# Four interleaved attention layers: VectorE's unspent allowance carried over, gates computed later, and some GpSimd copies moved to VectorE

## The chip, the cores and the metric

The kernel runs on one core of a Trainium2 chip. The metric is the device time of one execution in microseconds (us), lower is better. A core has five engines, each with its own queue, worked off in order: TensorE (PE, matmuls; its weight loads are listed as PEld), VectorE (DVE), ScalarE (ACT), GpSimd (POOL) and SyncE (SP, which here only issues DMA transfers). An instruction that needs another engine's result waits on a semaphore, and all that stands behind it in its queue waits too. TensorE writes to PSUM, eight banks of 128 x 512 fp32.

## What is computed

There are 2048 tokens of width 512, 32 heads of 16, and four residual layers in the order A, B, A, B, each on a layer norm of x.

```
B: q,k,v = x @ wqkv;  o = softmax(q k^T / 4) v over all 2048 keys;  o @ wo
A: four segments of 512 tokens, in each, per head:
     a_dot = softmax(q k^T / 4 + causal mask) v        (within the segment)
     a_mem = phi(q) M / (phi(q) z + 1e-6)              (memory of earlier segments)
     o = g * a_mem + (1 - g) * a_dot,   g = sigmoid(beta)
     M += phi(k)^T v ;  z += sum phi(k)
   o @ wo
phi(t) = t + 1 if t > 0 else exp(t)
```

In A the mask lets a query see only keys at or before its own position.

## The kernel before: how the work is laid out

All data stay on chip after the first loads. A planner in Python (class `Builder`) writes out the order of every engine's instructions before anything runs; a scheduler (`Sched`) adds the semaphore waits that the reads and writes need. Nothing is decided on the chip, so a change in the planner's rules moves instructions on all engines.

**A step.** The main loop (`attention`, L1189 on) advances in steps. A step takes up to three score tiles ("banks") of 128 keys x 512 queries, each of one head, from the groups that are selected. `unit` (L986) issues TensorE's score matmuls into PSUM banks 0 to 2 or 3 to 5, in turn, and one exponential on ScalarE for all three (L1039, PSUM to the SBUF tile pT). For A, GpSimd then zeroes what the causal mask forbids (L1054). Two steps later (three for A) TensorE multiplies pT with the values (`pv`, L1060) and adds into PSUM bank 6, the only accumulator. A group is the four heads of one residue and one 512-token query segment: 64 banks for B (fewer for partial key sets), 12 for A.

**The end of a group.** `finish` (L1081) has VectorE transpose the accumulator into the tile tT (L1099) or, for partial sums, copy or add it (L1090, L1092); only then may TensorE write bank 6 for the next group. VectorE takes reciprocals (L1103), in A it multiplies by the gate `omgT` (L1106), GpSimd scales the result into `ob` (L1112) and VectorE transposes that into `oT` (L1127).

**Masked queries.** A group's scores use a copy of the queries with the other heads' rows set to zero, the tile qm (L957). It is made when the group is selected, by VectorE for A groups and for groups that are needed at once, else by GpSimd.

**Exponentials on VectorE.** In addition to the three banks a step can take a fourth one for VectorE (`dx_pick`, L711): scores go to PSUM bank 7, VectorE converts them into fixed point (`dxt`, L748) and runs a chain of six instructions for one or two banks (`dx_chain`, L772 to L782) that gives the exponential's bits. At most total/6 banks of a group go this way (10 of 64), not in every step, and not while the planner's VectorE balance `cr_dve` is under -300.

**Background tasks and the balance.** Layer norm, projections, memory updates and output projections of other layers and segments run as generators between the steps (`background`). Each part names its cost, so many TensorE units and so many ns of VectorE. `credit` (L858) adds to the balances at each step: 1420 ns of VectorE for a step of B, 1300 for A, 2600 when work runs short. The balance is cut off at one step's amount, so what a step did not use is dropped.

**Memory and gates.** `task_mem` (L588) adds phi(k)^T v into M (L637, L639) and makes two copies masked per head, Mn and Mz (L643, L645, on GpSimd, 24 of each), which later matmuls read. `gates` (L421) computes the sigmoids gtok and omgT from beta: for each an exponential on ScalarE (L427) and two instructions on VectorE (L429, L430). It is called in the first segment's task (L553), behind the first layer norm and ahead of the first projections. The two small copies of beta are DMA transfers that SyncE issues behind the first weights (L381, L385).

TensorE's spare time is filled: `keep_busy` (L326) issues matmuls with a zero weight into bank 6, up to 1024 columns a step.

Of the kernel before, what the change touches and what calls it, by code (L numbers as in the profile page):

```python
# [5 lines left out]
ALU = mybir.AluOpType  # L6
# [168 lines left out]
def bcast(ap, dims):  # L175
    return bass.AP(tensor=ap.tensor, offset=ap.offset, ap=[list(ap.ap[0])] + [list(d) for d in dims])
# [36 lines left out]
class Builder:  # L213
# [326 lines left out]
    def task_A(self, L, s):  # L540
        sl = s % 2
        need = [("x", L, s)]
        if s >= 2:
            need += [("attn", L, s - 2), ("mem", L, s - 2)]
        if s == 0 and L > 0:
            need += [("attn", L - 2, 2), ("attn", L - 2, 3), ("mem", L - 2, 2), ("mem", L - 2, 3)]
        yield need, 0, 0
        k = yield from self.ln_part(L, s)
        yield ["xT"], 0, 0
        slot = self.take_xT()  # L550
        if L == 0 and s == 0:
            yield from self.ln_first(k, slot)
            self.gates()  # L553
        else:
            yield from self.ln_tiles(L, s, k, slot)
            yield [("dma", ("xT", L, s))], 0, 0
        for c in range(NCH):
            yield from self.proj_fm(self.wA, self.b_wA[1], 512, slot, c, self.KA[:, sl, c, :], self.b_KA[sl][c])
            self.flags.add(("K", L, s, c))
            yield from self.proj_fm(self.wA, self.b_wA[0], 0, slot, c, self.QA[:, sl, c, :], self.b_QA[sl][c])  # L560
            self.flags.add(("Q", L, s, c))
            if c == 0:
                for ti in range(4):
                    yield from self.proj_tm(self.wA, self.b_wA[2], 1024, slot, ti,
                                            self.v_evac(self.VA[:, sl, ti, :], self.b_VA[sl][ti]))
                self.flags.add(("V", L, s))
        if s < 3:
            prev = (L, s - 1) if s else (L - 2, 3)
            read = [("dma", ("amemT",) + prev + (3,))] if prev[0] >= 0 and prev[1] else []
            yield ([("mem",) + prev] if prev[0] >= 0 else []), 0, 0  # L570
            old = [o for b in self.b_phk for o in b.reads.values()]
            for c in range(NCH):
                self.dma_tr(self.phk[:, :, c * 128:(c + 1) * 128], self.KA[:, sl, c, :], [self.b_KA[sl][c]], [self.b_phkc[c]],
                            ("phk", L, s), old)
            for j in range(2):
                yield [("dma", ("phk", L, s))] + read, 0, 0
                a, ba = self.phk[:, 2 * j:2 * j + 2, :], self.b_phk[2 * j:2 * j + 2]
                yield from self.phi(a, self.b_phkc + ba, a, ba)
            self.flags.add(("phk", L, s))
        self.give_xT(slot)  # L580
        if s > 0:
            for c in (0, 2):
                yield [("op", L, s - 1), ("mem", L, s - 1)] + ([("dma", ("amemT", L, s - 1, 3))] if s > 1 else []), 0, 0
                yield from self.phi(self.QA[:, sl, c:c + 2, :], self.b_QA[sl][c:c + 2], self.phq[:, c:c + 2, :], self.b_phq[c:c + 2])
            self.flags.add(("phq", L, s))
        self.flags.add(("proj", L, s))

    def task_mem(self, L, s):  # L588
# [33 lines left out]
        if s < 3:  # L622
            for j in range(2):
                yield [("phk", L, s), ("V", L, s)], 2, 450
                bank, al = self.misc(), self.new_alloc()
                for cc in range(2):
                    c = 2 * j + cc
                    o = bank.col0 + cc * 136
                    for ti in range(4):
                        self.mm(self.ps[:, o:o + 136], self.phk[:, ti, c * 128:(c + 1) * 128],  # L630
                                self.VA[:, sl, ti, c * 136:(c + 1) * 136], ti == 0, ti == 3,
                                [self.b_phk[ti], self.b_VA[sl][ti]], bank, al)
                src = self.ps[:, bank.col0:bank.col0 + 272].rearrange("p (c h f) -> p c h f", c=2, f=17)
                M = self.M[:, 2 * j:2 * j + 2, :, :]
                bM = [self.b_M[j]]
                if s == 0:
                    self.op("dve", (lambda M, src: lambda e: e.tensor_copy(M, src))(M, src), writes=bM, bank=bank, alloc=al)  # L637
                else:
                    self.op("dve", (lambda M, src: lambda e: e.tensor_tensor(M, M, src, ALU.add))(M, src), reads=bM, writes=bM,  # L639
                            bank=bank, alloc=al)  # L640
            for c in range(NCH):
                hn = bcast(self.hmask[:, 0:1], [[1, 8], [0, 16]])
                self.op("pool", (lambda c, hn: lambda e: e.tensor_tensor(self.Mn[:, c, :, :], self.M[:, c, :, 0:16], hn, ALU.mult))(c, hn),  # L643
                        reads=[self.b_M[c // 2], self.b_hm], writes=[self.b_Mn])
                self.op("pool", (lambda c: lambda e: e.tensor_tensor(self.Mz[:, c, :], self.M[:, c, :, 16], self.hmask[:, :], ALU.mult))(c),  # L645
                        reads=[self.b_M[c // 2], self.b_hm], writes=[self.b_Mz])
        self.flags.add(("mem", L, s))

# [209 lines left out]
    def credit(self, pe, dve):  # L858

        self.cr_pe = min(self.cr_pe + pe, pe)  # L860
        self.cr_dve = min(self.cr_dve + dve, dve)

    def background(self, bank=None):
        while self.cr_dve > 0 and self.cr_pe > 0:
# [66 lines left out]
    def select(self, late):  # L931
        tail = self.sel[-2:]
        if len(self.sel) > 2 and self.seqA and self.seqA[0][0].L and all(g.kind == "B" and not g.pos for g in tail) and self.met(self.group_needs(self.seqA[0][0])):

            for g in tail:
                self.sel.remove(g)
                self.qm_free.insert(0, g.qm)
            self.seqB.insert(0, tail)
        while len(self.qm_free) > 1 and (len(self.sel) <= 1 or len(self.sel) == 2 and all(g.kind == "B" and g.total < 64 for g in self.sel)):
            pair = None  # L940
            for seq in (self.seqA, self.seqB):
                if seq and self.met(self.group_needs(seq[0][0])):
                    pair = seq.pop(0)
                    break
            if pair is None and self.seqB and sum(len(g.banks) - g.pos for g in self.sel) <= 6 and self.split():
                pair = self.seqB.pop(0)
            if pair is None:
                return
            for g in pair:
                g.qm = self.qm_free.pop(0)  # L950
                isA = g.kind == "A"
                q = (self.QA[:, g.qseg % 2, g.c, :] if isA else self.QB[:, g.qseg, g.c, :])
                bq = (self.b_QA[g.qseg % 2][g.c] if isA else self.b_QB[g.qseg][g.c])
                m = self.qm[:, g.qm, :]
                col = self.par[:, g.e:g.e + 1]
                eng = "dve" if late or isA else "pool"
                self.op(eng, (lambda m, q, col: lambda e: e.tensor_scalar(m, q, col, 0.0, op0=ALU.mult, op1=ALU.add))(m, q, col),  # L957
                        reads=[bq, self.b_par], writes=[self.b_qm[g.qm]])
                self.sel.append(g)
# [121 lines left out]
    def finish(self, g):  # L1081
# [20 lines left out]
        br = self.b_rd[m]  # L1102
        self.op("dve", lambda e: e.reciprocal(rd, tT[:, :, 16]), reads=[bt], writes=[br])  # L1103
        if g.kind == "A":
            om = self.omgT[:, g.c, g.e:g.e + 1]
            self.op("dve", lambda e: e.tensor_scalar(rd, rd, om, None, op0=ALU.mult), reads=[br, self.b_omgT], writes=[br])  # L1106
        if g.e == 0:
# [62 lines left out]
    def attention(self):  # L1170
# [18 lines left out]
        while True:  # L1189
# [23 lines left out]
            isA = items[0][0].kind == "A"  # L1213
# [5 lines left out]
            self.cr_dve -= self.pv_step(n)  # L1219
            self.run_deferred(False)  # L1220
            self.background(False if split else None)
            if self.step > 10:
                self.keep_busy()
            self.bg_cols = 0
# [49 lines left out]
```

## Time and profile before

| | us |
|---|---|
| three timed runs, median (lowest, highest) | 2142.66 (2138.74, 2143.29) |
| profiled execution, its own time | 2140.73 |
| its span, first to last instruction | 2138.6 |
| ScalarE busy | 2007.1 |
| TensorE matmuls busy | 1797.9 |
| VectorE busy | 1591.0 |
| GpSimd busy | 404.8 |
| ScalarE waited for TensorE before exponentials (L1039) | 88.3 |
| VectorE waited for TensorE before dxt (L748) | 88.1 |
| TensorE matmuls waited for tT (L1099), 51 times | 29.8 |
| TensorE matmuls waited for qm on GpSimd, 3 times | 8.3 |
| mean granted TensorE clock | 0.966 |

How to read it: in a group's line stand line of code, engine, operation, output<-input with shapes, count, then busy us and mean ns of one, then the engine's idle time ahead of these and whom it waited for. In a timeline the columns are start in us, duration, engine, line, operation, and in square brackets the idle time before it with its releaser; "x5" means that several instructions are drawn together, and the duration is then the stretch that they cover. In a table of windows each row is a stretch (start:end, length), then busy us and number of instructions of PE, PEld, DVE, ACT and POOL, then the granted TensorE clock as a share of full speed, the DMA engines' busy share and GB/s. Records of successive instructions of an engine can overlap, so the sum of the durations can exceed the busy time.

### The profile page before, as it was taken

The numbers are of one execution on the slowest core, as the hardware profiler recorded it, in microseconds if no ns is written. First come the engines' busy times: TensorE is split into PE (matmuls) and PEld (weight loads), VectorE is DVE, ScalarE is ACT, GpSimd is POOL, SyncE is SP. The second block draws the span as 40 slices with busy tenths as digits, with TensorE's granted clock in tenths as the row PEclk, the third lists the DMA queues.
The fourth block names the chain that finished last, engine by engine and source line by source line (L and its number), as shares of the span: only waits on it lengthen the run. The fifth ranks groups of instructions, "written<-read, shape, count | busy, mean of one in ns | idle before, by whom it ended". The sixth has DMA issues, their size and how long they took to land.

```text
span 2138.6 us, 34960 instructions
## 1 busy us (share of the span) xinstructions
PE 1797.9 (84%) x13626; PEld 497.4 (23%) x13726; DVE 1591.0 (74%) x2806; ACT 2007.1 (94%) x1618; POOL 404.8 (19%) x833
## 2 busy tenths in 40 slices
PE   7788888878888988889888888888888888888887
PEld 3222222222222222222222222222222222222222
DVE  6665665487658885688857975548899999989996
ACT  5689998999989999899998999999999999999997
POOL 3532533020150002400033102401100000000000
PEclk9899999999999999899988999999999999999999
DMA  4011100000000000000000001000000000000000
GB/s 138 11 30 21 21 11 11 11 1 13 9 1 11 1 13 9 11 11 1 16 11 6 1 1 21 11 11 1 11 1 1 1 11 1 1 1 11 1 1 11
DMA packets 67142, 24.81 MB, mean 12 GB/s; under 512 B 59808, under 2 KB 66464, under 8 KB 66976
## 3 DMA queue, kind: packets, MB, share of 16 engines
q1 hardware_dynamic: 66976, 22.57, 4.7%
q8 instruction: 108, 1.77, 0.3%
q14 instruction: 58, 0.48, 0.1%
HBM read 6.30 MB, written 2.10 MB: 4 GB/s over the span
## 4 chain that ended last, share of the span: by engine, by line
issue 38%; ACT 26%; PE 14%; DVE 6%; POOL 4%; DMA 0%; SPq 0%; POOLq 0%; ACTq 0%; DVEq 0%
ACT pT L1039 25%; PE ps L337 14%; POOL ob L1112 2%; POOL pT L1054 1%; POOL qm L957 1%; DVE tT L1099 1%; DVE dxt L748 1%; DVE VB L353 1%; DVE dxo L782 0%; DVE KB L353 0%; DVE x L702 0%; DVE QB L353 0%; DVE VA L353 0%; ACT amem L528 0%; DMA xT<-xn 0%
## 5 line engine op out<-in xcount | busy, mean ns | idle before, releaser
L1039 ACT ACTIVATE pT<-ps 128x1536 bf16<-128x1536 f32 (+2 forms) x1589 | 1984.9, 1547 | 103.6 <-PE ps L337 88.3
L337 PE MATMUL ps<-qm,KB 32*128 32x512 bf16 x4096 | 509.9, 387 | 206.6 <-ACT pT L1039 188.9
L337 PE MATMUL ps<-wB,zero 128*17 128x512 bf16 x2092 | 642.8, 390 | 0.0
L337 PE MATMUL ps<-pT,VB 128*17 128x512 bf16 x3716 | 496.8, 386 | 20.7 <-DVE tT L1099 15.3
L748 DVE TENSOR_SCALAR dxt<-ps 128x512 uint32<-128x512 f32 x380 | 261.1, 687 | 93.4 <-PE ps L337 88.1
L1112 POOL TENSOR_TENSOR ob<-tT,rd 128x256 bf16<-128x256 f32 x128 | 100.1, 782 | 1198.7 <-DVE rd L1103 1158.2
L337 PEld LDWEIGHTS ps<-qm,KB 32*128 32x128 bf16 x4096 | 126.8, 91 | 750.5 <-ACT pT L1039 653.0
L1054 POOL TENSOR_SCALAR_AFFINE_SELECT pT<-pT 128x256 bf16<-128x256 bf16 (+2 forms) x512 | 208.4, 423 | 331.3 <-ACT pT L1039 321.9
L782 DVE SCALAR_TENSOR_TENSOR dxo<-dxt,dxz 128x1024 int16<-128x1024 uint16 (+1 forms) x203 | 235.2, 1159 | 4.6
L337 PEld LDWEIGHTS ps<-wB,zero 128*17 128x17 bf16 x2092 | 179.5, 92 | 115.1 <-issue 7.7
L337 PEld LDWEIGHTS ps<-pT,VB 128*17 128x17 bf16 x3716 | 115.5, 87 | 349.2 <-issue 298.4
L337 PE MATMUL ps<-dxo,VB 128*17 128x512 bf16 x380 | 146.6, 386 | 0.1
L776 DVE TENSOR_TENSOR dxz<-dxz,dxo 128x1024 f16<-128x1024 f16 (+1 forms) x203 | 134.8, 664 | 4.3
L337 PE MATMUL ps<-qm,KA 32*128 32x512 bf16 (+3 forms) x1024 | 109.3, 330 | 33.3 <-ACT pT L1039 25.3
L772 DVE TENSOR_SCALAR dxo<-dxt 128x1024 f16<-128x1024 uint16 (+1 forms) x203 | 133.6, 658 | 3.4 <-PE ps L337 3.2
L780 DVE TENSOR_TENSOR dxz<-dxz,dxo 128x1024 f16<-128x1024 f16 (+1 forms) x203 | 131.8, 649 | 2.1
L1099 DVE STREAM_TRANSPOSE tT<-ps 128x512 f32<-128x512 f32 x112 | 79.6, 711 | 72.1 <-PE ps L337 69.9
L337 PE MATMUL ps<-pT,VA 128*17 128x512 bf16 (+3 forms) x1024 | 106.0, 334 | 22.0 <-DVE tT L1099 14.2
L957 POOL TENSOR_SCALAR qm<-QB,par 128x512 bf16<-128x512 bf16 x102 | 81.1, 802 | 174.6 <-PE ps L337 174.6
L774 DVE TENSOR_SCALAR dxz<-dxo 128x1024 f16<-128x1024 f16 (+1 forms) x203 | 88.4, 435 | 6.8
L778 DVE TENSOR_SCALAR dxz<-dxz 128x1024 f16<-128x1024 f16 (+1 forms) x203 | 83.3, 410 | 6.7
L702 DVE TENSOR_TENSOR x<-x,ps 128x512 bf16<-128x512 bf16 x64 | 44.0, 687 | 54.8 <-PE ps L337 54.8
(92 smaller groups left out, 1019.3 us busy)
## 6 DMA issues: line engine op xcount, KB each, us to landing
out_dram<-x SPq DMA_DIRECT2D x8, 256.0 KB, 2.1
x<-in_A_x_dram SPq DMA_DIRECT2D x3, 512.0 KB, 11.8
wB<-in_B_wqkv_dram SPq DMA_DIRECT2D x1, 1536.0 KB, 13.6
xT<-xn SPq DMA_TRANSPOSE x60, 2.4
x<-in_A_x_dram SPq DMA_DIRECT2D x4, 128.0 KB, 2.2
wA<-in_A_wk_dram SPq DMA_DIRECT2D x1, 512.0 KB, 4.1
wA<-in_A_wq_dram SPq DMA_DIRECT2D x1, 512.0 KB, 5.5
wA<-in_A_wv_dram SPq DMA_DIRECT2D x1, 512.0 KB, 6.4
```

The lines of the kernel that those rows point to most:

```text
L337: self.sc.add("pe", lambda e: e.matmul(out, lhsT, rhs, start=start, stop=stop, skip_group_check=True), reads=reads, banks=[(bank, "w", all ...
L748: self.op("dve", lambda e: e.tensor_scalar(self.dxt[:, b, i, :], o, SCALE * LOG2E * 65536, 127.0 * 65536, op0=ALU.mult, op1=ALU.add), writ ...
L772: self.op("dve", lambda e: e.tensor_scalar(f, lo, 2.0 ** -16, None, op0=ALU.mult), reads=bt, writes=bo)
L774: self.op("dve", lambda e: e.tensor_scalar(z, f, EXP_C3, EXP_C2, op0=ALU.mult, op1=ALU.add), reads=bo, writes=bz)
L776: self.op("dve", lambda e: e.tensor_tensor(z, z, f, ALU.mult), reads=bo + bz, writes=bz)
L780: self.op("dve", lambda e: e.tensor_tensor(z, z, f, ALU.mult), reads=bo + bz, writes=bz)
L782: self.op("dve", lambda e: e.scalar_tensor_tensor(ob, hi, 128.0, z, op0=ALU.mult, op1=ALU.add), reads=bt + bz, writes=bo)
L957: self.op(eng, (lambda m, q, col: lambda e: e.tensor_scalar(m, q, col, 0.0, op0=ALU.mult, op1=ALU.add))(m, q, col), reads=[bq, self.b_par] ...
L1039: self.sc.add("act", (lambda dst, src: lambda e: e.activation(dst, src, ACT.Exp, scale=SCALE))(dst, src), writes=self.b_pT[slot * 3 + i:sl ...
L1054: self.op("pool", (lambda blk, pat: lambda e: e.affine_select(blk, blk, pattern=pat, compare_op=ALU.is_ge, fill=0.0, base=0, channel_multi ...
L1099: self.op("dve", lambda e: e.transpose(tT.rearrange("p a b -> p (a b)"), src), reads=bsrc, writes=[bt], bank=bk, alloc=al)
L1112: self.op("pool", lambda e: e.tensor_tensor(ob, tT[:, :, 0:16], rb, ALU.mult), reads=[bt, br], writes=[self.b_ob[oi][g.e]])
```

## The change

It has four edits.

1. `gates()` is no longer called in the first segment's task. The main loop calls it once, at the end of step 2. An assertion says that omgT has been written when `finish` uses it.
2. The masked copies Mn and Mz are made by VectorE instead of GpSimd, and each of the four pairs is announced to the planner as 500 ns of VectorE work.
3. The VectorE balance may exceed a step's amount by 1200 ns: what a step leaves unused is kept up to that limit.
4. A masked query of a B group is made by VectorE if a group of A is among those selected, else by GpSimd as before.

```diff
@@ task_A
         if L == 0 and s == 0:
             yield from self.ln_first(k, slot)
-            self.gates()
@@ task_mem
             for c in range(NCH):
                 hn = bcast(self.hmask[:, 0:1], [[1, 8], [0, 16]])
-                self.op("pool", (... self.Mn[:, c, :, :], self.M[:, c, :, 0:16], hn, ALU.mult ...
+                yield [], 0, 500
+                self.op("dve", (... self.Mn[:, c, :, :], self.M[:, c, :, 0:16], hn, ALU.mult ...
-                self.op("pool", (... self.Mz[:, c, :], self.M[:, c, :, 16], self.hmask[:, :], ALU.mult ...
+                self.op("dve", (... self.Mz[:, c, :], self.M[:, c, :, 16], self.hmask[:, :], ALU.mult ...
@@ credit
         self.cr_pe = min(self.cr_pe + pe, pe)
-        self.cr_dve = min(self.cr_dve + dve, dve)
+        self.cr_dve = min(self.cr_dve + dve, dve + 1200)
@@ select
-                eng = "dve" if late or isA else "pool"
+                eng = "dve" if late or isA or any(h.kind == "A" for h in self.sel) else "pool"
@@ finish
         if g.kind == "A":
+            assert self.b_omgT.last_write is not None and self.step > 2
@@ attention
             self.background(False if split else None)
+            if self.step == 2:
+                self.gates()
```

More of the change, by code (lines that the diff above doesn't have):

```diff
@@ L642, in task_mem @@
                 hn = bcast(self.hmask[:, 0:1], [[1, 8], [0, 16]])
-                self.op("pool", (lambda c, hn: lambda e: e.tensor_tensor(self.Mn[:, c, :, :], self.M[:, c, :, 0:16], hn, ALU.mult))(c, hn),
+                yield [], 0, 500
+                self.op("dve", (lambda c, hn: lambda e: e.tensor_tensor(self.Mn[:, c, :, :], self.M[:, c, :, 0:16], hn, ALU.mult))(c, hn),
                         reads=[self.b_M[c // 2], self.b_hm], writes=[self.b_Mn])
-                self.op("pool", (lambda c: lambda e: e.tensor_tensor(self.Mz[:, c, :], self.M[:, c, :, 16], self.hmask[:, :], ALU.mult))(c),
+                self.op("dve", (lambda c: lambda e: e.tensor_tensor(self.Mz[:, c, :], self.M[:, c, :, 16], self.hmask[:, :], ALU.mult))(c),
                         reads=[self.b_M[c // 2], self.b_hm], writes=[self.b_Mz])
```

## The prediction

> **What bounds the kernel now.** I read the page's busy shares first, then the groups with their shapes kept apart, then busy time in stretches of 100 us.
>
> ```profile
> PE 1797.9 (84%) x13626; PEld 497.4 (23%) x13726; DVE 1591.0 (74%) x2806; ACT 2007.1 (94%) x1618; POOL 404.8 (19%) x833
> ```
> ```profile
> L1039 ACT ACTIVATE pT<-ps 128x1536 bf16<-128x1536 f32 x1366 | 1857.8, 1686 | 81.1 <-PE ps L337 71.0 <-POOL pT L1054 4.1 <-POOL ob L1112 2.5
> ```
> ```profile
> 100.00:200.00 100.00, 85.02 (x605) 24.24 (x614) 60.32 (x126) 83.11 (x72) 32.24 (x77) 0.90 0.11 22
> ...
> 1700.00:1800.00 100.00, 84.13 (x666) 22.21 (x664) 92.45 (x144) 100.00 (x75) 7.98 (x8) 1.00 0.02 6
> ```
>
> ScalarE (ACT) sets the time: in the late stretch it is busy for 100 of 100 us with VectorE (DVE) at 92, and 60 of 100 early. Exponential records overlap, so 1686 ns is not the price of one: layer 3's third query segment runs from 1725.8 to 1927.7 us in 149 steps of three banks, 1.355 us a step. That is the price of a step below. ScalarE stands idle 122 us in all, 16 of them before the first exponential. Three of its longest later waits look like this one in the timeline:
>
> ```profile
> 871.09 2.35 POOL L1054 TENSOR_SCALAR_AFFINE_SELECT pT<-pT 128x384 bf16<-128x384 bf16 x5 [0.82 <-ACT pT L1039]
> ...
> 873.40 0.62 POOL L1112 TENSOR_TENSOR ob<-tT,rd 128x256 bf16<-128x256 f32 x1
> 874.00 1.36 POOL L957 TENSOR_SCALAR qm<-QB,par 128x512 bf16<-128x512 bf16 x2
> 874.81 0.10 PEld L337 LDWEIGHTS ps<-qm,KB 32*128 32x128 bf16 x1 [3.64 <-issue]
> 874.84 0.58 PE L337 MATMUL ps<-qm,KB 32*128 32x512 bf16 x1 [3.37 <-POOL qm L957]
> ...
> 876.04 0.60 ACT L1039 ACTIVATE pT<-ps 128x512 bf16<-128x512 f32 x1 [3.55 <-PE ps L337]
> ```
>
> GpSimd (POOL) makes the masked queries behind five causal masks; TensorE (PE) waits 3.37 us for them and ScalarE 3.55. The last view is the opposite case, a group's end in the late stretch, first in the timeline, then in windows of 3.41 us:
>
> ```profile
> 1576.27 0.68 DVE L748 TENSOR_SCALAR dxt<-ps 128x512 uint32<-128x512 f32 x1
> ...
> 1576.88 0.70 DVE L1099 STREAM_TRANSPOSE tT<-ps 128x512 f32<-128x512 f32 x1
> ...
> 1577.63 0.61 PE L337 MATMUL ps<-pT,VB 128*17 128x512 bf16 x4 [0.74 <-DVE tT L1099]
> ...
> 1579.74 1.45 ACT L1039 ACTIVATE pT<-ps 128x1536 bf16<-128x1536 f32 x1 [0.60 <-PE ps L337]
> ```
> ```profile
> 1573.99:1577.41 3.42, 2.06 (x17) 0.48 (x14) 3.32 (x7) 3.42 (x4) 0.00 (x0) 1.00 0.00 0
> 1577.41:1580.82 3.41, 3.19 (x14) 0.61 (x14) 2.79 (x5) 2.81 (x3) 2.87 (x3) 0.51 0.02 5
> ```
>
> The only accumulator bank must be transposed by VectorE (L1099) before the next group may write it. TensorE waited 0.74 us, was busy for 2.06 of 3.42 us, and in the next window its granted clock is 0.51; ScalarE then waits 0.60 us.
>
> **The change part by part.** Steps, banks and instructions are counted from the order that the planner of each kernel writes out; durations are the rows of before. For VectorE I use the pitch, from one start to the next where less than 0.1 us lies between.
>
> *1. Allowance kept (L861).* The planner hands 424 banks to VectorE's exponential where it handed over 380. The exponentials on ScalarE fall from 1239 steps of layers 1 and 3 to 1224, so 15 x 1.355 = **-20.3 us**. (44 banks by columns: 44/3 x 1.355 = 19.9.)
>
> VectorE pays for each bank one L748 (0.606) and for each chain 0.692 + 0.448 + 0.696 + 0.382 + 0.676 + 1.225 = 4.119 us (L772 to L782); chains go from 203 to 227. 44 x 0.606 + 24 x 4.119 = 125.6 us. It all lies beside ScalarE as long as VectorE has room.
>
> *2. Masked queries and masked copies to VectorE.* 20 queries move (0.353 us each, the row of L957 on VectorE): 7.1 us. Mn (24 of 128x128) and Mz (24 of 128x8) have no VectorE row. By the nearest rows Mn lies between 0.20 (128 of the 272 columns of L639's 0.44) and 0.40 (GpSimd's own), and Mz between 0.13 (L446's pitch) and 0.20 (GpSimd's own). I take 0.30, near the median 0.29 of L606, the same shape, and 0.16: 11 us of VectorE time. With part 1 that makes +144 us on 1618 in pitches.
>
> What it removes are the waits like 874.00. There are three (616, 874 and 1137 us), with 2.48 + 3.55 + 3.55 = 9.6 us of ScalarE's idle time at once and half a clock behind them. In the windows 611.5 to 627, 869.5 to 885.5 and 1131 to 1148.5 ScalarE is busy 31.1 of 49.0 us, idle 17.9. GpSimd's ob and causal masks remain and are next late. Ends: 0 and -17.9. I take two thirds, **-12 us**; VectorE idles over 3 us at these very places.
>
> *3. Later gates (L553).* The gates wait for the small beta transfer in front of the first copies:
>
> ```profile
> 16.04 0.21 ACT L427 ACTIVATE omgT<-betT 128x8 f32<-128x8 bf16 x1 [5.09 <-DMA betT<-in_A_beta_dram]
> ...
> 17.56 0.61 PE L337 MATMUL ps<-qm,KA 32*128 32x512 bf16 x3 [4.70 <-DVE qm L957]
> ```
>
> The projections that the copies need end at 12.86. From there: ACT's copy 0.58, two queries 0.61, a start near 13.9 instead of 17.56: -3.6. The half clock from 17.6 to 24.4 follows that wait, so some more may go. The two exponentials (0.44 us together) come back after step 2. At most -6, at least 0, if the x tiles behind the first four are late; I take **-4.5**.
>
> *4. What VectorE's fuller queue costs.* VectorE work a step by stage, in pitches, against 1355 ns: layer 1's query segments 1 to 3 go from 1125, 1116, 1164 to 1226, 1209, 1274; layer 3's from 1272, 1236, 1227 to **1348, 1348, 1248**. Two stages, 296 steps, have no room left. Unused allowance used to be dropped; now up to 1.2 us comes at once, ahead of the transposition in the same queue.
>
> I added up, step by step, VectorE's work less 1355 ns (not below zero). Before, 0.4 to 0.6 us stands ahead of a group's end in the attention stages; after, 1.3 to 5.9. Where the transposition comes late by more than ScalarE's cover, the excess is lost and the queue drains as much. With 1.4 us of cover (step and a bit) the excess sums to 16.7 us against 4.3 before; with 0.6 (the wait of 1577, where the clock falls) to 37.6 against 5.9. So it costs 12 to 32 us, and 2 to 14 if all pitches are 4% shorter. I take **+18**, below the middle, as early layer-1 steps take 1.5 us, not 1.355.
>
> Here the clock counts. The TensorE page of the Trainium skill ("TensorE: Matmul & The Clock Gate", section "Why this matters for your kernels") says that gaps under about 3 us do not cost the clock. By that, item 4 would be 12 us and the whole sum 2118. The rows disagree: 0.74 us of waiting sufficed.
>
> **Sum:** -20.3 - 12 - 4.5 + 18 = -18.8 us. The profiled execution took 2140.7 (span 2138.6), so 2121.9; the median of the runs shown is 1.9 higher, so **2124**.
>
> **The rivals.**
> - *Short waits keep the clock* and VectorE's lateness costs 2 to 12: -20.3 - 12 - 4.5 + 2 or + 12, so 2108 to 2118. For it: 6 windows less than 60% busy were not followed by half a clock. Against: 27 drops, most after windows 40 to 65% busy. The Trainium skill's rule would make this one true.
> - *VectorE's lateness costs nothing and all the GpSimd waits go*: -20.3 - 17.9 - 6, 2098. For it: at 92% in the late stretch ScalarE still did not wait.
> - *The gains cancel*: 32 us of lateness, and of the GpSimd waits only the 9.6 us at once are saved, -20.3 - 9.6 - 4.5 + 32 = -2.4: 2140.
> - *VectorE becomes the bound, slower*: place, the segments at 1348 ns and the group ends of layer 1; price, if pitches come out 4% longer (1402 over 1355), the same sum gives 68 to 82 us, less 5 to 8 of before, so +60 to +75 against -36.8: 2166 to 2180. It decides from about 2% (57 - 7 = 50: 2156). For it: chains with GpSimd running show longer L772 (0.86 to 0.92 instead of 0.68). Against: in the late stretch of before, pitches gave VectorE's occupied time within 1.5%.
> - *The allowance stays unused*: excluded, the changed order has 424 banks.
>
> **How the numbers follow.** Forecast 0.48 (own range 2112 to 2134), clock kept 0.12, nothing lost 0.12, cancelled 0.10, VectorE bound 0.18. No more than 2 in 10 left out: from 2098 (the second rival's own time) to 2160, which takes in the start of the last. A measurement here tells 0.2%, 4.3 us: faster 0.72 (the first three), same 0.09, slower 0.19.
>
> **What would show it.** ScalarE with 1568 exponentials instead of 1589; VectorE near 1730 us busy; no wait on qm from GpSimd at a group's end; the first exponential near 14.5 us. TensorE's waits for tT (58.9 us now, both its queues) should grow; item 4 is right if idle time of ScalarE in layers 1 and 3 attention grows by 10 to 30 us, and wrong below 5. If VectorE is busy above 97% in layer 3's segments and a step there takes over 1.39 us, the slower rival has come.

## The result and the profile after

| | before | after |
|---|---|---|
| median of the timed runs, us | 2140.7 (2135.6 to 2143.3) | 2192.7 (2189.5 to 2194.8) |
| ratio, 95% interval | | 1.0245 (1.0222 to 1.0267) |
| span of the profiled execution, us | 2138.6 | 2193.1 |

The change costs 2.4%. The forecast was 2124, and the range ended at 2160: both are wrong. One execution of the experiments below, the profiled one of `allow600`, took 4699 us and is left out together with its trace. The page of the changed kernel answers with these lines: busy time, the chain that ended last by engine, then the exponentials with shapes kept apart.

```profile
PE 1819.4 (83%) x13605; PEld 500.3 (23%) x13708; DVE 1713.7 (78%) x3060; ACT 1999.6 (91%) x1597; POOL 379.3 (17%) x765
...
issue 37%; DVE 26%; PE 20%; ACT 11%; POOL 4%; DMA 1%; SPq 0%; POOLq 0%; DVEq 0%; ACTq 0%
```
```profile
L1039 ACT ACTIVATE pT<-ps 128x1536 bf16<-128x1536 f32 x1352 | 1850.5, 1582 | 141.5 <-PE ps L337 128.6 <-POOL ob L1113 3.6 <-POOL pT L1054 2.7
```

In the kernel before the chain was this:

```profile
issue 38%; ACT 26%; PE 14%; DVE 6%; POOL 4%; DMA 0%; SPq 0%; POOLq 0%; ACTq 0%; DVEq 0%
```

ScalarE has less to do, as planned, but its wait for TensorE ahead of full exponentials went from 71.0 to 128.6 us, and in the chain VectorE stands for 26% where it stood for 6, ScalarE for 11 instead of 26. VectorE is busy for 78% only: a bound by its total is not what this says.

Where the time went is found by the start of the first exponential of each stage. Layer 1's query segments 1 to 3 take 57 us more (629.8 to 686.8 us), its segment 0 takes 8.7 more; layer 0 is 3.0 us shorter, layer 2 is 4.4 us shorter, and layer 3 takes 843 us in both, with seven steps fewer. The start gained 3.8 us. The same attention stage of layer 1, 100 us of it, before and then after, in the table of windows:

```profile
630.00:730.00 100.00, 88.23 (x665) 24.44 (x672) 83.73 (x142) 99.96 (x75) 5.75 (x12) 1.00 0.04 6
```
```profile
640.00:740.00 100.00, 82.81 (x548) 22.15 (x555) 75.53 (x127) 84.56 (x63) 5.26 (x11) 0.93 0.03 6
```

63 exponentials instead of 75, and *every* engine has become idler, VectorE too. Nothing is saturated here; the engines wait for one another. The timeline of the changed kernel shows how, in one place of that stage:

```profile
697.05 0.43 DVE L774 TENSOR_SCALAR dxz<-dxo 128x1024 f16<-128x1024 f16 x1
697.18 0.55 PEld L337 LDWEIGHTS ps<-wB,xT 128*128 128x128 bf16 x4 [0.23 <-DVE dxo L772]
697.18 1.04 PE L337 MATMUL ps<-wB,xT 128*128 128x512 bf16 x4
697.51 0.69 DVE L776 TENSOR_TENSOR dxz<-dxz,dxo 128x1024 f16<-128x1024 f16 x1
...
698.24 0.43 DVE L778 TENSOR_SCALAR dxz<-dxz 128x1024 f16<-128x1024 f16 x1
...
698.70 0.69 DVE L780 TENSOR_TENSOR dxz<-dxz,dxo 128x1024 f16<-128x1024 f16 x1
699.31 0.69 DVE L353 CAST VB<-ps 128x512 bf16<-128x512 f32 x1
700.05 0.39 PE L337 MATMUL ps<-qm,KB 32*128 32x512 bf16 x1 [1.19 <-DVE VB L353]
...
701.62 1.45 ACT L1039 ACTIVATE pT<-ps 128x1536 bf16<-128x1536 f32 x1 [1.20 <-PE ps L337]
```

TensorE ends a projection in PSUM bank 7 at 698.22. VectorE could empty the bank at once, but four chain instructions stand ahead of that eviction in its queue, and at 698.22 two of them (L778 and L780) are still to run; it starts at 699.31. The next matmul for bank 7, a score bank for VectorE, waits 1.19 us, TensorE's queue behind it waits too, and so ScalarE waits 1.20 us.

### The profile page after: what moved, and what is told of

It is laid out like the page before. It is cut to its first block, busy times and chain, and to the rows that moved or that the text cites. A ratio compares the mean times of both kernels' runs of the same rounds, so it can differ in the third digit from the quotient of the medians.

```text
span 2193.1 us, 35007 instructions
## 1 busy us (share of the span) xinstructions
PE 1819.4 (83%) x13605; PEld 500.3 (23%) x13708; DVE 1713.7 (78%) x3060; ACT 1999.6 (91%) x1597; POOL 379.3 (17%) x765
## 4 chain that ended last, share of the span: by engine, by line
issue 37%; DVE 26%; PE 20%; ACT 11%; POOL 4%; DMA 1%; SPq 0%; POOLq 0%; DVEq 0%; ACTq 0%
PE ps L337 20%; ACT pT L1039 10%; DVE dxt L748 3%; DVE dxo L782 3%; DVE dxz L776 2%; DVE dxo L772 2%; POOL ob L1113 2%; DVE dxz L780 2%; DVE tT L1099 1%; POOL pT L1054 1%; DVE dxz L774 1%; POOL qm L957 1%; DVE dxz L778 1%; DVE lnst L444 1%; DVE x L702 1%
## 5 line engine op out<-in xcount | busy, mean ns | idle before, releaser
L1039 ACT ACTIVATE pT<-ps 128x1536 bf16<-128x1536 f32 (+3 forms) x1568 | 1976.1, 1461 | 164.5 <-PE ps L337 150.1
L337 PE MATMUL ps<-qm,KB 32*128 32x512 bf16 x4096 | 538.2, 392 | 189.3 <-ACT pT L1039 149.1
L748 DVE TENSOR_SCALAR dxt<-ps 128x512 uint32<-128x512 f32 x424 | 290.5, 685 | 74.2 <-PE ps L337 71.4
L782 DVE SCALAR_TENSOR_TENSOR dxo<-dxt,dxz 128x1024 int16<-128x1024 uint16 (+1 forms) x227 | 263.6, 1161 | 4.2
L337 PE MATMUL ps<-dxo,VB 128*17 128x512 bf16 x424 | 164.2, 391 | 0.4 <-DVE dxo L782 0.4
L776 DVE TENSOR_TENSOR dxz<-dxz,dxo 128x1024 f16<-128x1024 f16 (+1 forms) x227 | 150.6, 663 | 5.8
L772 DVE TENSOR_SCALAR dxo<-dxt 128x1024 f16<-128x1024 uint16 (+1 forms) x227 | 150.6, 663 | 5.3 <-PE ps L337 3.5
L780 DVE TENSOR_TENSOR dxz<-dxz,dxo 128x1024 f16<-128x1024 f16 (+1 forms) x227 | 150.8, 664 | 5.0
L957 POOL TENSOR_SCALAR qm<-QB,par 128x512 bf16<-128x512 bf16 x82 | 72.1, 886 | 185.8 <-PE ps L337 182.9
L778 DVE TENSOR_SCALAR dxz<-dxz 128x1024 f16<-128x1024 f16 (+1 forms) x227 | 94.8, 418 | 6.1
L337 PE MATMUL ps<-xT,wB 128*128 128x512 bf16 x230 | 72.5, 416 | 21.5 <-DMA xT<-xn 4.8
```

What stands on the lines that cost most here:

```text
L337: self.sc.add("pe", lambda e: e.matmul(out, lhsT, rhs, start=start, stop=stop, skip_group_check=True), reads=reads, banks=[(bank, "w", all ...
L748: self.op("dve", lambda e: e.tensor_scalar(self.dxt[:, b, i, :], o, SCALE * LOG2E * 65536, 127.0 * 65536, op0=ALU.mult, op1=ALU.add), writ ...
L772: self.op("dve", lambda e: e.tensor_scalar(f, lo, 2.0 ** -16, None, op0=ALU.mult), reads=bt, writes=bo)
L776: self.op("dve", lambda e: e.tensor_tensor(z, z, f, ALU.mult), reads=bo + bz, writes=bz)
L778: self.op("dve", lambda e: e.tensor_scalar(z, z, EXP_C1, None, op0=ALU.add), reads=bz, writes=bz)
L780: self.op("dve", lambda e: e.tensor_tensor(z, z, f, ALU.mult), reads=bo + bz, writes=bz)
```

## The experiments

Three theories were to be told apart. *Bank 7* ("theory 1" in the expectations below): only replies for the shared bank are late, because a bank for VectorE and a background matmul come in neighbouring steps. *Amount* (the prediction's slower rival, "rival 2" below): VectorE has too much work, most of all in layer 3. *Queue* (formed after the first four runs, "theory 3" below): the kept balance is spent in one go, so VectorE's queue is longer whenever TensorE needs a reply, at bank 6 and bank 7. "Banks" are those handed to VectorE. The kernel before was timed again beside each set of runs (medians 2139.9 to 2143.7 us), and the ratios are to these; differences of medians between sets are good to a few us only.

**One edit undone, one edit alone.** `no_allow` is the changed kernel with the old balance, `allow_only` the kernel before with the new one.

```diff
-        self.cr_dve = min(self.cr_dve + dve, dve + 1200)
+        self.cr_dve = min(self.cr_dve + dve, dve)
```

> The changed kernel with the balance cut off at one step's amount again (one line undone); later gates, masked queries and masked copies as changed. 377 banks on VectorE, 1496 steps. Theory 1 (the allowance alone costs time) and the prediction's items 2 and 3: about 16 us faster than before, 2118 to 2132. Rival (the moved copies and queries load VectorE and cost time themselves): 2145 or more.

> The kernel before with one line changed: the balance may keep 1200 ns. 424 banks on VectorE, 1480 steps, 45 of the banks in the step behind a background matmul task that uses the same PSUM bank 7 (12 before). Theory 1: all of the loss and none of the gains of the other edits, 2195 to 2215. Rival (the other edits cost a part): between 2150 and 2185.

Measured: `no_allow` 2118.2 us, ratio 0.987 (0.984 to 0.990); `allow_only` 2206.0, 1.0288 (1.0263 to 1.0313). The kept allowance does all of the harm, and the other edits gain more than the 16 us of the prediction's items 2 and 3. In `no_allow` the stage shown above is as it was:

```profile
630.00:730.00 100.00, 88.83 (x670) 24.19 (x669) 84.12 (x142) 99.80 (x75) 4.40 (x9) 1.00 0.03 6
```

**Less kept, and bank 7 guarded on one side.** `allow300` keeps 300 ns; `guard_dx` keeps 1200:

```diff
-        if self.low or ... or self.step - self.dx_step < (2 if not self.pending() ...
+        if self.low or ... or self.step - self.bank_step < 2 or self.step - self.dx_step < (2 if not self.pending() ...
```

> The changed kernel with 300 ns kept instead of 1200. 408 banks on VectorE, 1486 steps, 9 neighbours on bank 7. Theory 1: 2115 to 2135, since neither a long queue nor neighbours come about. Rival 2: the loss goes with the banks handed over, 28 of 44, so 2155 to 2180.

> The changed kernel, allowance kept, but a bank goes to VectorE only if no background task has used PSUM bank 7 in the step before. 414 banks on VectorE, 1484 steps, 4 instead of 45 such neighbours. Theory 1 (the eviction of bank 7 stands behind chain instructions, TensorE waits for it in order): most of the loss goes, 2115 to 2140. Rival 2 (VectorE has too much work and is late at the ends of groups): 34 of the 44 additional banks remain, so 2170 to 2190.

Measured: `allow300` 2129.7, 0.9941 (0.9921 to 0.9962); `guard_dx` 2200.0, 1.0255 (1.0222 to 1.0287). The bank-7 theory in this form fell: 4 such neighbours instead of 45, and no gain. But the guard did not remove the waits at bank 7. TensorE's weight loads waited longer for dxt than in the changed kernel, first the changed kernel, then `guard_dx` (engine, whom it waited for, us, times, longest):

```profile
PEld ps L337 <- DVE dxt L748: 47.2, 70, 1.9
PEld ps L337 <- DVE dxt L748: 75.2, 102, 2.0
```

The amount theory fell with the other run: `allow300` hands over 408 banks, 31 more than `no_allow`, and is 11 us slower than that, where this theory expected 2155 to 2180.

**Guarded on both sides.** In addition no background matmul follows a bank for VectorE in the next step (`self.step == self.dx_step` becomes `self.step - self.dx_step < 2`).

> The changed kernel, allowance kept, but no bank goes to VectorE in the step after a background task that uses PSUM bank 7, and no such task runs in the step after a bank for VectorE: 4 and 0 such neighbours instead of 45 and 60. 366 banks on VectorE, 1500 steps. If the loss is made at bank 7 alone: 2118 + 4 steps more = 2120 to 2135, TensorE's waits for dxt near nothing. Theory 3 (every reply of VectorE comes late, at bank 6 too): half of the loss stays, 2145 to 2170, with the waits for tT and the partial sums as long as in the changed kernel.

Measured: 2191.4, 1.0236 (1.0219 to 1.0252), slower than either theory gave, the queue theory too. Its page:

```profile
PE 1842.8 (84%) x13764; PEld 503.2 (23%) x13764; DVE 1581.5 (72%) x2852; ACT 2016.8 (92%) x1611; POOL 376.7 (17%) x769
```

VectorE has *less* work here than before the change (1581.5 against 1591.0 us, 366 banks against 380), yet the kernel is about 50 us slower. In layer 1's attention stages the waits of TensorE's weight loads for dxt are 8 us instead of 39, but those for the transposition of bank 6 (26) and for the partial sums (19) are as long as in the changed kernel (27 and 18). This does not clear bank 7, though: in layer 3 the waits for dxt are 21 us where the changed kernel has 8. Set against `no_allow`, `guard_both` loses 31 us in layer 1, where the changed kernel loses 56, and 22 in layer 3, where the changed kernel loses 3. So the guard took away a good part of layer 1's loss, and other loss came in its place; what the guard itself costs is open, as no kernel has it without the allowance.

**In which layers.** `self.layer` is the layer of the step's first bank.

```diff
-        self.cr_dve = min(self.cr_dve + dve, dve + 1200)
+        self.cr_dve = min(self.cr_dve + dve, dve + (1200 if self.layer < 3 else 0))     # allow_early
+        self.cr_dve = min(self.cr_dve + dve, dve + (1200 if self.layer == 3 else 0))    # allow_late
```

> The changed kernel with the 1200 ns kept only in steps of layers 0 to 2; in layer 3 the balance is cut off as before. 409 banks on VectorE. Theory 3 (a longer VectorE queue makes TensorE wait for every reply, and only where background matmuls leave TensorE no slack, in layer 1, is the wait lost): nearly the whole loss, 2175 to 2195. Rival (VectorE is saturated in layer 3, 1348 of 1355 ns): most of the loss goes, 2120 to 2140.

> The changed kernel with the 1200 ns kept only in steps of layer 3. 393 banks on VectorE, 1492 steps, 4 fewer than with no allowance kept (2118.2). Theory 3: 2112 to 2122, the steps saved against a few us of lateness. Rival (saturation in layer 3): 2150 or more.

Measured: `allow_early` 2194.4, 1.0245 (1.0215 to 1.0274): the whole loss. `allow_late` 2133.1, 0.9959 (0.9947 to 0.9971): 15 us more than `no_allow`, more than expected, with 5 steps fewer. So the saturated stages of layer 3, the place that the prediction named, are not where the kernel loses most.

**How much is kept.**

> The changed kernel with 600 ns kept. 409 banks on VectorE and 1485 steps, as good as with 300 ns (408, 1486; 2129.7). If the number of banks sets the loss: 2126 to 2134 again. If the length of VectorE's queue does (theory 3): between the values for 300 and 1200 ns, 2142 to 2170.

> The changed kernel with 2400 ns kept. 422 banks on VectorE and 1481 steps, as good as with 1200 ns (424, 1480; 2192.7). If the number of banks sets the loss: 2188 to 2198 again. Theory 3: still longer waits of TensorE for every reply, 2205 to 2250.

Measured: `allow600` 2164.8, 1.0111 (1.0087 to 1.0136); `allow2400` 2243.0, 1.0465 (1.0433 to 1.0497). With nearly equal numbers of banks (408 and 409; 424 and 422) the time rises by 35 and 50 us. Both times lie in the range of the queue theory, and the number of banks does not set the loss.

**Who spends it.** The part above one step's amount is `self.carry`; in `carry_dx` only VectorE's exponentials may use it, in `carry_bg` only background tasks.

```diff
+        self.carry = max(0, self.cr_dve - dve)
 carry_dx:
-  ... self.cr_dve + slack < pick["next"][2]
+  ... self.cr_dve - (0 if pick is self.dx_task else self.carry) + slack < pick["next"][2]
 carry_bg:
+  ... self.cr_dve - (self.carry if pick is self.dx_task else 0) + slack < pick["next"][2]
-  ... or self.cr_dve < -300 or ...
+  ... or self.cr_dve - self.carry < -300 or ...
```

> The changed kernel with 1200 ns kept, but the kept part is only for the exponentials (their banks and chains); background tasks see the balance cut off at one step's amount. 407 banks on VectorE, 1486 steps, like the kernel with 300 ns (408; 2129.7). If it is chain instructions that stand ahead of VectorE's replies: 2165 to 2195. If it is background work (layer norms, evictions) that is sent in bursts: 2118 to 2135.

> The changed kernel with 1200 ns kept, but the kept part is only for background tasks; banks and chains see the balance cut off. 400 banks on VectorE, 1488 steps. If chain instructions ahead of the replies do the harm: 2115 to 2135. If bursts of background work do: 2160 to 2190. If both share it, this and the other kernel lie between, 2140 to 2165.

Measured: `carry_dx` 2189.2, 1.0228 (1.0209 to 1.0248), nearly the whole loss with 407 banks, 60 us more than `allow300` with 408 (2991 instructions on VectorE against 2986); `carry_bg` 2141.9, 1.0010 (0.9997 to 1.0024), 24 us more than `no_allow`. The kept balance in the hands of the exponentials does most of it, background work does a part of its own.

**What one number orders them.** For each kernel I counted the steps of layer 1 in which the planner sends VectorE over 2.0 us of work, in the pitches of before; a step lasts about 1.36 us.

| kernel | kept, ns | banks | steps | such steps | median, us |
|---|---|---|---|---|---|
| no_allow | 0 | 377 | 1496 | 9 | 2118.2 |
| allow300 | 300 | 408 | 1486 | 14 | 2129.7 |
| carry_bg | 1200 | 400 | 1488 | 24 | 2141.9 |
| allow600 | 600 | 409 | 1485 | 29 | 2164.8 |
| carry_dx | 1200 | 407 | 1486 | 65 | 2189.2 |
| guard_both | 1200 | 366 | 1500 | 69 | 2191.4 |
| after | 1200 | 424 | 1480 | 75 | 2192.7 |
| guard_dx | 1200 | 414 | 1484 | 82 | 2200.0 |
| allow2400 | 2400 | 422 | 1481 | 97 | 2243.0 |

The time follows this column through these nine kernels, and no other column. No expectation had named the count, and it has limits: with 1.8 us in place of 2.0 the order is broken, and of the two kernels that are not in the table `allow_early` plans layer 1 as the changed kernel does and takes the same time, but `allow_late` plans it as `no_allow` does and takes 15 us more. It is no proof of a price for one such step.

**The other edits alone.** Each is put into the kernel before.

```diff
 gates_only:   self.gates() moved to the end of step 2
 qm_only:      eng = "dve" if late or isA or any(h.kind == "A" for h in self.sel) else "pool"
 mn_only:      Mn, Mz on "dve", with  yield [], 0, 500  ahead of each pair
```

> The kernel before with the gates called at the end of step 2 and nothing else. The prediction's item 3: the first exponential 3.6 us earlier and 4 us off the time, 2137 to 2140. Rival (what the start gains is lost again in the first groups, as TensorE's clock and the transfers set their pace): no difference, within 2 us, with the first exponential still 3.6 us earlier.

> The kernel before, with the masked queries behind causal groups made by VectorE and nothing else; same banks and steps as before. The prediction's item 2: the three waits of 2.4 to 3.4 us on GpSimd go, with the half clock behind them: 12 to 18 us faster, 2124 to 2130. Rival (GpSimd's masks and ob are next late): 0 to 5 us.

> The kernel before, with the masked copies Mn and Mz made by VectorE, 500 ns announced for each pair, and nothing else. 377 banks on VectorE, one step more. The prediction gave this no time of its own: within 3 us of before, 2139 to 2145. Rival (the copies stood in GpSimd's way between the causal masks, so that layer 2's groups gain): 5 to 10 us faster.

Measured: `gates_only` 2137.8, 0.9984 (0.9970 to 0.9997), about 3.4 us; `qm_only` 2130.6, 0.9950 (0.9930 to 0.9971), 10.7 us, a little less than expected; `mn_only` 2125.3, 0.9931 (0.9906 to 0.9957), 14.7 us, which neither the expectation nor its rival held. Together 28.8 us, and `no_allow`, which has all three, gains 27.8 (0.013 of 2140): they add up. With the allowance they do not: the changed kernel, which has all four edits, is only about 9 us faster than `allow_only` (1.0245 against 1.0288). `mn_only` gains 14.0 us in layer 2's four causal stages and 4.2 in layer 0's, and loses 7.9 in layer 1. It changes the engine of the copies and, through the announced 500 ns, the order of other work; which of these two brings the gain was not tried apart.

## Why the prediction was wrong

*Bound and price of a step: right.* Where nothing is late a step still takes 1.34 us (layer 3's segments 1 and 2 in `no_allow`, 200.2 us for 149 steps).

*Item 1, -20.3 us: the count was right* (1480 steps, 424 banks, 1568 exponentials, VectorE 1714 us busy). The steps were saved, but the time was not; what they are worth by themselves no run shows.

*Item 3, -4.5 us: right.* In the changed kernel the two copies no longer wait for beta:

```profile
12.91 0.60 ACT L351 ACTIVATE QA<-ps 128x512 bf16<-128x512 f32 x1 [2.38 <-PE ps L337]
...
13.95 0.39 PE L337 MATMUL ps<-qm,KA 32*128 32x512 bf16 x3 [1.08 <-DVE qm L957]
...
14.39 2.79 ACT L1039 ACTIVATE pT<-ps 128x1536 bf16<-128x1536 f32 x2 [0.88 <-PE ps L337]
```

The first score matmul starts at 13.95 (13.9 was forecast), and alone the edit is worth 3.4 us.

*Item 2: the queries right* (-12 forecast, 10.7 alone). TensorE waits less where GpSimd made them, as here in the changed kernel, though not nothing:

```profile
907.39 2.14 POOL L1054 TENSOR_SCALAR_AFFINE_SELECT pT<-pT 128x384 bf16<-128x384 bf16 x5 [0.82 <-ACT pT L1039]
907.97 0.97 DVE L957 TENSOR_SCALAR qm<-QB,par 128x512 bf16<-128x512 bf16 x2
...
908.71 0.60 PE L337 MATMUL ps<-qm,KB 32*128 32x512 bf16 x1 [0.94 <-DVE qm L957]
...
909.93 0.60 ACT L1039 ACTIVATE pT<-ps 128x512 bf16<-128x512 f32 x1 [1.14 <-PE ps L337]
```

*The masked copies, counted at nothing but VectorE time, gained 14.7 us*: a term that was missing, on the good side.

*Item 4 is the step that failed*: "where the transposition comes late by more than ScalarE's cover, the excess is lost and the queue drains as much", +18 us. The kept balance costs 74.5 us by the medians of the changed kernel and `no_allow` (80 by their ratios, 62 in `allow_only`), although it saves 16 steps of 1.355, 21.7 us; so the lateness costs about 96 us (82 to 102 by the other two figures), against the 12 to 32 that were given. By stage, 56 of the 74.5 us lie in layer 1 and 19 in layer 2. The sign that item 4 had named, 10 to 30 us more idle time of ScalarE in the attention of layers 1 and 3, was overrun: 60 us more in layer 1 (16.2 to 76.2) and 8 in layer 3 (21.7 to 29.9). Two assumptions were wrong.

- *That 0.6 to 1.4 us of each wait is covered.* In layer 1's attention stages TensorE's waits for VectorE, summed over its weight loads, rise from 66 to 150 us: dxt from 5 to 39, projections from 23 to 38, tT from 13 to 27, partial sums from 12 to 18, output projections from 4 to 14. These 84 us more go with 66 us of time lost there and 8 steps (10.8 us) saved, 77 in all: little of the waiting was covered. In layer 3 the waits rise by 17 us and 9.5 are lost. Why layer 1 has so little cover stays open. Background matmuls are a possible reason, as layer 1's segments 1 to 3 have 88 to 128 of them each and layer 3's 16; but layer 1's segment 0 has 318 and lost 8.7 us only.
- *That the transposition is the reply that counts.* The running sum looked for backlog that piles up over many steps, and found most in layer 3. What goes with the loss are short bursts: over 2.0 us of VectorE work in one step of layer 1, 5 times before and 75 after. From the start of TensorE's last weight load to the start of VectorE's read, the mean delay in layer 1 grew from 0.61 to 0.96 us at bank 7 and from 0.68 to 1.15 at bank 6. At bank 7 the median stays at 0.63: a part of the replies is late, by much. Those for bank 7 are the most frequent, 322 against 56.

The waits of the changed kernel show it in two rows (engine, whom it waited for, us, times, longest):

```profile
PE ps L337 <- DVE tT L1099: 48.2, 52, 2.5
PEld ps L337 <- DVE dxt L748: 47.2, 70, 1.9
```

The same rows before:

```profile
PE ps L337 <- DVE tT L1099: 29.8, 51, 1.7
PEld ps L337 <- DVE dxt L748: 6.0, 22, 0.6
```

The transposition is waited for just as often, only longer; dxt is a wait that hardly existed.

*The clock.* Item 4 weighed a rule of the Trainium skill ("TensorE: Matmul & The Clock Gate", section "Why this matters for your kernels"): the page warns of gaps of TensorE over about 3 us, and the prediction read it as shorter gaps costing no clock. That does not hold here: of the 37 drops to half clock in the changed kernel only one has such a gap in the two windows of 3.41 us ahead of it. The windows at half clock rise from 42 to 52 (29 in `no_allow`). In layer 1's attention stages the time at half clock rises from 14 to 80 us, and of the 60 us more that ScalarE idles there 25 lie in it. So the clock has a part in the loss, less than half of it by this count; no run tells a wait apart from the slower clock that follows it.

*The slower rival had the sign and not the mechanism.* "VectorE becomes the bound" was given 0.18 and 2166 to 2180, with its place in layer 3's segments and at layer 1's group ends and its price from VectorE's work a step. VectorE's share is 78%, and 94% in layer 3's segment 1 (193.22 of 206.00 us), where the rival had named 97% as its sign; `guard_both` loses nearly as much with less VectorE work than before, and `allow_early` loses everything without layer 3. Layer 1's group ends were the right place for a part: the waits for tT doubled there. The chance of 0.72 for faster hung on a sum that charged for amounts, where what changed was the order.

`no_allow`, three of the four edits, is faster than both kernels: 2118.2 us.

## What to carry to other kernels

An engine with idle time is not an engine with room: if others wait for its replies in order, the length of its queue at the moment of the reply decides, and spreading its work evenly (a balance that forgets what was not used) can be worth more than filling it. Test an allowance by its dose with the amount of work held equal; here 300 and 600 ns hand over 408 and 409 banks and lie 35 us apart. And test edits of a bundle one at a time: three of these four were worth 28 us, the fourth hid it, and beside it they gained about 9 only.

## What was not expected of the hardware

With all engines waiting for each other, every busy share fell at once (ScalarE 99.96 to 84.56, VectorE 83.73 to 75.53, TensorE 88.23 to 82.81 in the windows above), so these shares do not point at the engine whose queue is late. And moving small work, 24 copies of 0.40 us and 24 of 0.20 on GpSimd, to VectorE gave 14.7 us together with the 500 ns announced for each pair, more than the 14.4 us that the copies take together.
